# One long convolution and a token mixer on one core: the last step's spectra of x by way of DRAM, the mixer's first statistics inside the convolution's order, and the order itself

## The chip, the cores and the metric

The kernel runs on one core of a Trainium2 chip. A core has four engines that compute: PE (TensorE) multiplies matrices into PSUM, DVE (VectorE), ACT (ScalarE) and POOL (GpSimd) work elementwise. SP (SyncE) issues the DMAs. Each engine takes its instructions in the order in which they stand in its queue and waits on semaphores for the others. The metric is the time of one execution in microseconds (us).

## The reference

```python
def reference(A_u, A_log_A_real, A_A_imag, A_C_real, A_C_imag, A_log_dt, A_D_skip, B_x, B_w1, B_w2, B_w3, B_w4):
    ...
        A = -jnp.exp(log_A_real) + 1j * A_imag
        C = (C_real + 1j * C_imag) * dt[:, None]
        P = jnp.exp((A * dt[:, None])[:, :, None] * pos[None, None, :])
        K = 2.0 * jnp.einsum("dn,dnl->dl", C, P).real
        Kf = jnp.fft.rfft(K, L2)
        Uf = jnp.fft.rfft(u_t, L2)
        y = jnp.fft.irfft(Uf * Kf[None, :, :], L2)[:, :, :L]
        return y + u * D_skip[None, None, :]
    ...
        h = _gelu(_layernorm(x, axis=-1) @ w1)
        ...
        x1 = x + hs
        h2 = _gelu(_layernorm(x1, axis=-1) @ w3) @ w4
        return x1 + h2

    x = A_u
    h = x + _A_ref(_layernorm(x, axis=-1), ...)
    h2 = h + _B_ref(_layernorm(h, axis=-1), ...)
    return h2
```

The sequence has 2048 places and 512 channels, in float32. The first half makes for each channel a filter as long as the sequence out of 128 decaying oscillations, and convolves the normed input with it by Fourier transforms. The second half is a mixer: layer norm, a product with w1, gelu, four shifted groups of channels, a product with w2, then layer norm, w3 (512 to 1792), gelu and w4.

## The kernel before

The convolution (`conv_phase`) goes over the channels in four steps of 128, numbered 0 to 3. Each step has these parts.

- **Tables and taps.** For every 16 channels (32 groups in all, eight a step) `table` makes the oscillations' factors: POOL adds phases (`pt`), ACT takes sines and cosines of them, DVE and POOL multiply with the amplitudes `amx` and `amp` into the tables `cs` and `sn`. `taps` multiplies the tables on PE into `kt`, the taps of the filter. Which group's `amp`, second half of `cs` (`csy`) or of `sn` (`sny`) is POOL's and which is DVE's stands in the table `SHARE`.
- **Spectra of the taps, first stage.** Either `stage_a_turn`, two groups of matmuls (`kt,fas`) for 64 channels and four half transposes on DVE (`at<-bank`, 128x512), or `stage_a_taps`, many small matmuls (`fas,kt`) and copies by ACT. `TURN64` says which 64 channels are turned.
- **Spectra of x, first stage.** `stage_a_x`: matmuls of the normed input h (`h,fas`), and four wide transposes on DVE (`at<-bank`, 128x1024). Once x of a step is read, four DMAs load the raw input into its place in h again, for the residual.
- **Second stage and product.** The buffer `at` has two halves, of x and of the taps. In steps 0 to 2 `product` takes both through the second stage at once, eight times (`at,tbs` into `bank`, 128x256): ACT copies x's spectrum into `xs`, and DVE multiplies it with the taps' spectrum into `u`. In step 3 `spectrum_x` takes x alone ahead of the taps (`at,tbs` 128x128), and ACT keeps the eight results in `xs`, in `scratch` and in `p8`; `product` then takes the taps alone. In step 3 DVE also adds the products in pairs (`u<-u`), so that the inverse takes two terms and not four.
- **The way back.** `stage_b_inv` (`u,ms`, then a copy into `at` by ACT, eight times), `turn_inv` (four transposes on DVE), `stage_a_inv` (`u,fis`), which adds the old h either on PE, by a matmul with the identity (`h,ident`), and lets ACT copy the sum, or on DVE. The last step ends in `last_a_inv`: four pieces of 512 rows, `at,fis` on PE, added into h by DVE, in the order 3, 0, 1, 2.

x of all steps is normed once, in the head (`norm_x`): DVE takes 5 of 16 rows, ACT 11.

What sets the order: every operation goes with a cost, its keys read and written, and for some a due time (`at=`) to a planner, `Plan`. It walks through a model of the engines and always starts what can start first, among equals what is due first. The due times come from the numbers `NOM`. PSUM banks are given out by the planner as well, and where PE would be idle long, it places dummy matmuls with the identity (`filler`). The planner's result is a fixed order for each engine; on the chip each queue runs in this order. SP's DMAs are ordered by it too.

The mixer's phase stands behind it in written order: `finish(3)` takes the statistics of the last 512 rows' second half, `norms([3])` their root by a dozen short DVE operations, `norm1(3)` makes the normed rows `xl`, PE runs nine dummy matmuls (`warm`) and transposes `xl` (`xt`), and then come the products `l` with w1. Its end is a loop over 14 blocks of w3 and w4.

All instructions bear the line of a recording helper (L88 before, L87 after), so that the profile is read by tile names.

Of the kernel before, what the change touches and what calls it, by code (L numbers as in the profile page):

```python
# [287 lines left out]

@with_exitstack
def conv_phase(ctx, tc, cst, tp, h, x, log_A_real, A_imag, C_real, C_imag, log_dt, D_skip, w1, w2, fa, fi, tb, mm_):  # L290
# [422 lines left out]
    def stage_a_x(s, r):  # L713
# [47 lines left out]

    def spectrum_x(s, e):
        n = 4 * WID[s]
        dst, keys = slot(s, e)
# [4 lines left out]
        add("ACT", 0.22 + n * 0.51e-3, lambda: act.copy(dst[:, 0:n], plan.view(p)[:, 0:n]), w=keys, frees=p)

    def product(s, e):
# [735 lines left out]
```

## Time and profile before

| | us |
|---|---|
| median of 3 runs | 735.42 (733.86 to 735.68) |
| the profiled execution | 735.98, span 734.1 |
| convolution, to the mixer's first product | 338.5 |
| the mixer from there | 395.6 |
| busy over the span: PE, DVE, ACT, POOL | 677.4, 543.9, 411.9, 354.6 |

A row of a timeline has its start and length in us, the engine, the line, the operation, out<-in, the shapes and how often it follows itself; in brackets stands how long the engine was idle before it, and what ended that. A row of groups has the count, busy us, mean ns of one, and idle time before. One matmul of float32 is recorded as two rows, so that x16 is eight instructions.

### The profile page before, as it was taken

The page shows a single profiled execution, that of the slowest core. Times are in us where ns is not written, and L with a number is a line of the kernel's source. Part 1 is how long each engine was busy: PE and PEld are TensorE (multiplying, and loading weights), DVE is VectorE, ACT ScalarE, POOL GpSimd, SP SyncE. Part 2 cuts the span into 40 slices and gives each one's busy share as a digit, 9 for nine tenths or more (in the row PEclk, how much of TensorE's full clock was granted, in tenths as well). Part 3 has the DMA queues.
Part 4 walks back from the last instruction along what each step waited for, and adds up shares of the span by engine and source line. Part 5 has one row for each costly group of instructions (what it writes and reads, how often), then busy time and mean ns, then how long its engine had stood idle before and what let it go on. Part 6 is the DMA issues. An engine that isn't in the chain of part 4 may idle for free.

```text
span 734.1 us, 17022 instructions
## 1 busy us (share of the span) xinstructions
PE 677.4 (92%) x7096; PEld 523.4 (71%) x7096; DVE 543.9 (74%) x954; ACT 411.9 (56%) x710; POOL 354.6 (48%) x345
## 2 busy tenths in 40 slices
PE   1997599899988988998999999999999999999997
PEld 1886457537635761867888777888888888888886
DVE  5999899988898988669645689765657965445444
ACT  7687878868966872324744436573535554343430
POOL 0797677477785635001245533543345655444410
PEclk9999789999998998999999999999999999999999
DMA  7920020002001102201001101211122152111014
GB/s 182 312 85 17 3 59 3 17 3 60 18 2 40 25 15 59 59 1 58 1 1 29 30 1 30 71 44 46 41 57 58 45 148 82 47 54 45 13 29 115
DMA packets 40365, 36.82 MB, mean 50 GB/s; under 512 B 4448, under 2 KB 31072, under 8 KB 40288
## 3 DMA queue, kind: packets, MB, share of 16 engines
q1 hardware_dynamic: 39520, 34.68, 17.2%
q10 hardware_dynamic: 768, 1.05, 0.6%
q8 instruction: 56, 0.92, 0.5%
q14 instruction: 21, 0.17, 0.1%
HBM read 31.53 MB, written 4.19 MB: 49 GB/s over the span
## 4 chain that ended last, share of the span: by engine, by line
PE 63%; DVE 15%; ACT 13%; issue 3%; DMA 3%; SPq 1%; POOL 1%; ACTq 0%; DVEq 0%; POOLq 0%
PE l L88 19%; PE bank L88 14%; PE acc L88 10%; ACT pt L88 8%; DVE u L88 3%; DVE sn L88 3%; DVE cs L88 2%; PE l3c L88 2%; PE l3f L88 2%; PE l3d L88 2%; PE l3g L88 2%; PE l3e L88 2%; PE l3a L88 2%; PE l3b L88 2%; DVE at L88 1%
## 5 line engine op out<-in xcount | busy, mean ns | idle before, releaser
L88 ACT ACTIVATE pt<-pt 128x1056 f32<-128x1056 int32 x64 | 69.5, 1086 | 15.2 <-DVE cs L88 8.2
L88 POOL TENSOR_TENSOR pt<-p,s 128x1024 int32<-128x1024 int32 x32 | 63.5, 1989 | 23.8 <-DVE sn L88 20.0
L88 PE MATMUL bank<-at,tbs 128*64 128x256 f32 (+1 forms) x640 | 61.0, 339 | 4.0 <-ACT at L88 3.4
L88 PE MATMUL bank<-u,ms 64*128 64x128 f32 x896 | 56.7, 278 | 3.6 <-DVE u L88 3.3
L88 PEld LDWEIGHTS bank<-u,ms 64*128 64x128 f32 x896 | 52.0, 188 | 7.7 <-DVE u L88 4.9
L88 PEld LDWEIGHTS bank<-at,tbs 128*64 128x64 f32 x640 | 39.2, 134 | 22.4 <-ACT at L88 5.3
L88 PEld LDWEIGHTS bank<-ident 128*128 128x128 f32 x362 | 46.8, 209 | 5.6 <-issue 3.1
L88 PE MATMUL bank<-ident 128*128 128x128 f32 x362 | 50.5, 297 | 0.0
L88 DVE TENSOR_TENSOR cs<-pt,amx 128x512 f32<-128x512 f32 x64 | 41.3, 679 | 6.1 <-ACT pt L88 3.3
L88 DVE TENSOR_TENSOR h<-h,l 128x512 f32<-128x512 f32 x48 | 32.6, 686 | 14.9 <-PE l L88 14.8
L88 DVE TENSOR_TENSOR u<-u,l3f 128x512 f32<-128x512 f32 x14 | 9.6, 684 | 44.9 <-PE l3f L88 44.9
L88 POOL TENSOR_TENSOR cs0w<-raw,cs0w 128x512 fp32r<-128x512 f32 x7 | 9.1, 1301 | 67.0 <-ACT cs0w L88 58.3
L88 POOL TENSOR_TENSOR cs<-pt,amp 128x512 f32<-128x512 f32 x26 | 31.7, 1220 | 16.1 <-ACT pt L88 13.5
L88 POOL TENSOR_TENSOR cs1w<-raw,cs1w 128x512 fp32r<-128x512 f32 x7 | 9.1, 1297 | 61.5 <-ACT cs1w L88 61.5
L88 PE MATMUL bank<-sn 128*32 128x64 f32 x1024 | 32.0, 223 | 6.9 <-DVE sn L88 6.3
L88 ACT ACTIVATE pt<-pt,halfpi 128x1056 f32<-128x1056 f32 x32 | 37.8, 1182 | 0.2
L88 DVE TENSOR_TENSOR u<-xs,bank 128x1024 f32<-128x1024 f32 x26 | 31.5, 1216 | 8.3 <-ACT xs L88 8.0
L88 DVE STREAM_TRANSPOSE at<-bank 128x512 f32<-128x512 f32 (+1 forms) x36 | 33.0, 947 | 6.4 <-PE bank L88 6.3
L88 ACT COPY at<-bank 128x512 f32<-128x512 f32 x44 | 26.7, 616 | 19.2 <-PE bank L88 19.0
L88 ACT ACTIVATE u<-u 128x512 f32<-128x512 f32 x56 | 35.4, 633 | 1.8
L88 PE MATMUL bank<-cs 128*32 128x64 f32 x1024 | 33.2, 225 | 2.8 <-issue 1.1
L88 PEld LDWEIGHTS bank<-cs 128*32 128x32 f32 x1024 | 24.2, 111 | 16.0 <-issue 6.8
(1155 smaller groups left out, 2093.2 us busy)
## 6 DMA issues: line engine op xcount, KB each, us to landing
raw<-in_B_w_dram SPq DMA_DIRECT2D x28, 256.0 KB, 2.8
h<-in_A_u_dram SPq DMA_DIRECT2D x32, 128.0 KB, 4.0
h<-in_A_u_dram SPq DMA_DIRECT2D x16, 256.0 KB, 4.5
rawa<-in_B_w_dram SPq DMA_DIRECT2D x14, 256.0 KB, 2.9
rawb<-in_B_w_dram SPq DMA_DIRECT2D x14, 256.0 KB, 2.9
ms<-in_mm_dram SPq DMA_DIRECT2D x4, 768.0 KB, 11.0
out_dram<-h SPq DMA_DIRECT2D x48, 64.0 KB, 1.7
tbs<-in_tb_dram SPq DMA_DIRECT2D x4, 512.0 KB, 6.5
```

Source lines behind the costliest of these rows:

```text
L88: ins = f(*args, **kw)
```

## The change

Six things change in the convolution.

1. `FAR = [3]`: step 3's x is transformed (`stage_a_x`, then `spectrum_x` eight times) in the head, between the norm and step 0's x. ACT copies each spectrum into one of four buffers (`xs`, `u`, by turns), and a DMA of 256 KB stores it in DRAM (`far`). `back` loads it into the place in `xs`, `scratch` or `p8` from which step 3 multiplies.
2. The sums of products, so far made in step 3 alone, are made for single products of steps 0, 1 and 2 too, on DVE or on POOL (`sum0` to `sum3` in `SHARE`): fifteen in all and not eight, eight of them on POOL.
3. `TURN64` becomes `turn` in `SHARE`: seven of eight groups of 64 channels are turned, and not five. `HADD` becomes `hadd` by halves of a step: half of step 2 has its h added on PE and copied by ACT.
4. `KEEP`: in the last step the old h goes into the sum by identity matmuls ahead of `at,fis`, and ACT copies the four pieces of h; DVE added them before.
5. The statistics of the last 512 rows and their root (`norms`, now a function that both phases use) are handed to the planner.
6. `SHARE` and `NOM` have new numbers, so that the order is another on every engine.

```diff
-SHARE = {'amy': [[2, 5, 6, 7], [0, 1, 2, 3, 4, 5, 7]], 'csy': [[1, 3, 4, 6, 7], [0, 1, 2, 3, 4, 5, 7]], 'sny': [[1, 3, 4, 6, 7], [0, 4, 6, 7]], 'sq': [[1, 4, 5, 7], [0, 2, 4, 6]]}
+SHARE = {'amy': [[2, 3, 5, 6, 7], [0, 1, 2, 3, 4, 5, 6, 7]], 'csy': [[1, 3, 4, 7], [0, 1, 2, 3, 4, 5, 7]], 'sny': [[1, 3, 4, 7], [0, 2, 4, 6, 7]], 'sq': [[0, 1, 2, 7], [1, 2, 3, 4, 6]], 'turn': [[0, 1, 2, 4, 5, 6, 7], [1, 6, 7]], 'hadd': [[0, 1, 2, 3, 5, 7], [0, 2, 5, 7]], 'sum0': [[0], [0]], 'sum1': [[2, 4], []], 'sum2': [[4], [1, 2, 4, 6]], 'sum3': [[0, 1, 2, 3, 5, 6, 7], [1, 4, 7]]}
...
+FAR = [3]
...
-TURN64 = [[0], [0], [0], [0, 1]]
...
-HADD = [True, True, False]
-AHEAD = 8
-KEEP = False
+KEEP = True
...
+def norms(nc, cst, qs):
+
+    ra, rb, rr, nb = cst["norm"]
+    mv, t = cst["mv"], slice(qs[0] * 4, qs[-1] * 4 + 4)
+    return [
+        lambda: nc.vector.tensor_scalar(ra[:, 0, t], mv[:, t, 1], EPS, None, ALU.add),
...
+        *rsqrt_ops(nc, None, None, rr[:, :, t], ra[:, :, t], rb[:, :, t]),
...
+    dpool = pool("far", 1, space=bass.MemoryType.DRAM)
...
+    far = {(s, e): dpool.tile([128, 4 * W], F32, name=f"far{s}{e}") for s in FAR for e in RE}
+
     def spectrum_x(s, e):
         n = 4 * WID[s]
+        k = e % 4
+        dst, keys = (xs[k], [("xs", k)]) if k < XS else (uu[k - XS], [("u", k - XS)])
+        p = add("PE", 0.02 + n * 1.97e-3, lambda: stage_b(s, e, 0, plan.view(p)), dense=DB,
+                r=[("a0", e, q) for q in range(8)] + [("tb", e // 2)], w=keys, bank=1, at=NOM["xa"] + NOM["xs"] * FAR.index(s) + 16 + 2 * e)
+        add("ACT", 0.22 + n * 0.51e-3, lambda: act.copy(dst[:, 0:n], plan.view(p)[:, 0:n]), w=keys, frees=p)
+        add("SP", 0.8, dma(far[s, e][:, 0:n], dst[:, 0:n]), r=keys, w=[("far", s, e)])
+
+    def back(s, e):
+        n = 4 * WID[s]
         dst, keys = slot(s, e)
...
+        add("SP", 0.8, dma(dst[:, 0:n], far[s, e][:, 0:n]), r=[("far", s, e)], w=keys, at=TS[s] + e * NOM["b"] * WID[s] / 128 - 20)
...
+        eng = "POOL" if e in SHARE[f"sum{s}"][1] else "DVE" if e in SHARE[f"sum{s}"][0] else None
...
+            add(eng, 2 * dve(2 * w_) if eng == "DVE" else 1.3, sums, w=[uk], port=True)
...
+        summed = any(e in c for c in SHARE[f"sum{s}"])
+        terms = ((0, 0), (2, 1)) if summed else ((0, 0), (1, 3), (2, 1), (2, 2))
...
+    for n, s in enumerate(FAR):
+        for r in range(WID[s] // 32):
+            stage_a_x(s, r, NOM["xa"] + NOM["xs"] * n)
+        for e in RE:
+            spectrum_x(s, e)
     for r in range(WID[0] // 32):
-        stage_a_x(0, r)
+        stage_a_x(0, r, TS[0] - NOM["ax"])
...
-        for e in range(AHEAD) if last else ():
-            spectrum_x(s, e)
+        for e in RE if last else ():
+            back(s, e)
...
+    add("DVE", 1.8, lambda: finish(3), r=[("hq", 3)] + [("bs", j) for j in range(12, 16)], w=["mv"], at=TS[NS])
+    add("DVE", 2.75, norm_h, r=["mv"], w=["norm"], at=TS[NS])
+    plan.filler = busy
+    plan.run()
...
-    finish(3), norms([3])
     nc.scalar.activation(zero, zero, AF.Gelu_apprx_tanh)
```

The order of the instructions at three places, before and now.

SP's queue in the head, behind the loads of the constants `fis`, `tbs` and `ms`; `ec` is the load of a quarter of w1, h the reload of raw input. Before:

```order
L331 DMA fis<-in_fi_dram 128x64
L331 DMA tbs<-in_tb_dram 128x1024 x4
L331 DMA ms<-in_mm_dram 128x3x512 x4
L331 DMA ec<-in_B_w_dram 128x4x128
L331 DMA h<-in_A_u_dram 32x16x128 x4
```

Now:

```order
L344 DMA ms<-in_mm_dram 128x3x512 x4
L344 DMA ec<-in_B_w_dram 128x4x128
L344 DMA h<-in_A_u_dram 32x16x128 x2
L344 DMA far_125<-xs_123 128x512
L344 DMA far_127<-u_121 128x512
L344 DMA h<-in_A_u_dram 32x16x128
L344 DMA far_124<-xs_122 128x512
L344 DMA far_126<-u_120 128x512
L344 DMA h<-in_A_u_dram 32x16x128
L344 DMA far_129<-xs_123 128x512
L344 DMA far_131<-u_121 128x512
L344 DMA far_128<-xs_122 128x512
```

Eight stores (four from each pair of buffers, `far_130` follows) stand on the queue among the four reloads of step 3's h, where only step 0's reloads stood.

DVE at the end of the last step (`u` the products and their sums, `mvh` the moments of h). Before:

```order
L88 TENSOR_TENSOR u_118<-u_118 128x256 x2
L88 TENSOR_TENSOR u_119<-p_106,bank_81 128x1024
L88 TENSOR_TENSOR u_119<-u_119 128x256 x2
L88 TENSOR_TENSOR u_118<-p_106,bank_82 128x1024
L88 TENSOR_TENSOR u_118<-u_118 128x256 x2
L88 STREAM_TRANSPOSE at<-at 128x16x2x32 x4
L88 TENSOR_TENSOR h<-h,bank_81 128x4x128
L88 TENSOR_TENSOR h<-h,bank_82 128x4x128
L88 TENSOR_TENSOR h<-h,bank_81 128x4x128
L88 TENSOR_TENSOR h<-h,bank_82 128x4x128
L88 BN_STATS bs<-h 128x6 x4
L88 BN_AGGR mvh<-bs 128x2 x4
```

Now:

```order
L87 TENSOR_TENSOR u_121<-u_121 128x256 x2
L87 TENSOR_TENSOR u_120<-scratch,bank_84 128x1024
L87 TENSOR_TENSOR u_121<-p_108,bank_83 128x1024
L87 TENSOR_TENSOR u_120<-p_108,bank_83 128x1024
L87 TENSOR_TENSOR u_120<-u_120 128x256 x2
L87 STREAM_TRANSPOSE at<-at 128x16x2x32 x4
L87 BN_STATS bs<-h 128x6 x4
L87 BN_AGGR mvh<-bs 128x2 x4
```

The four adds of h have left DVE, and two of the last four products have no sums behind them there (POOL makes them). ACT has the copies of h, behind its last copies into `at`; it loaded its next function table there before. Now on ACT:

```order
L87 COPY h<-bank_83 128x16x32
L87 COPY at<-bank_81 128x4x64x2 x8
L87 COPY h<-bank_84 128x4x128
L87 COPY h<-bank_83 128x4x128
L87 COPY h<-bank_82 128x4x128
L87 COPY h<-bank_81 128x4x128
L87 ACT_TABLE_LOAD
L87 ACTIVATE zero<-zero 128x1
```

More of the change, by code (lines that the diff above doesn't have):

```diff
@@ L706, in spectra_of_taps @@
         for r in range(WID[s] // 64):
-            if r in TURN64[s]:
+            if 2 * s + r in SHARE["turn"][0]:
                 stage_a_turn(s, r)
@@ L727, in stage_a_x @@
         keys = [("a0", e, c) for e in RE for c in (2 * r, 2 * r + 1)]
-        p = add("PE", 1.2, mm, dense=0.9, r=[("h", s, r), "fas"] + prm(s), w=keys, bank=2, at=TS[s] - NOM["ax"] + 3.5 * r)
+        p = add("PE", 1.2, mm, dense=0.9, r=[("h", s, r), "fas"] + prm(0), w=keys, bank=2, at=nom + 3.5 * r)
         add("DVE", 1.15, tr, w=keys, frees=p)
@@ L776, in product @@
         a1 = [("a1", q, j) for q in range(w_ // 32) for j in range(2)]
-        if s + 1 == NS and e < AHEAD:
+        if s in FAR:
             p = add("PE", 0.02 + n * 1.97e-3, lambda: stage_b(s, e, 1, plan.view(p)), dense=DB, r=a1 + [("tb", e // 2)],
@@ L804, in product @@
         add("DVE", 0.07 + 2 * n * 1.1e-3, mult, r=keys, w=[uk], frees=p)
-        if s + 1 == NS and e >= YE:
+        eng = "POOL" if e in SHARE[f"sum{s}"][1] else "DVE" if e in SHARE[f"sum{s}"][0] else None
+        if eng:
+            en = gp if eng == "POOL" else v
             q = u[:, 0 : 2 * n].rearrange("p (i n) -> p i n", i=4)
             def sums():
-                v.tensor_tensor(q[:, 0], q[:, 0], q[:, 3], ALU.subtract)
-                v.tensor_tensor(q[:, 1], q[:, 1], q[:, 2], ALU.add)
-            add("DVE", 2 * dve(2 * w_), sums, w=[uk], port=True)
+                en.tensor_tensor(q[:, 0], q[:, 0], q[:, 3], ALU.subtract)
+                en.tensor_tensor(q[:, 1], q[:, 1], q[:, 2], ALU.add)
+            add(eng, 2 * dve(2 * w_) if eng == "DVE" else 1.3, sums, w=[uk], port=True)
     def stage_b_inv(s, e):
@@ L1006, in conv_phase @@
             weights()
-        for e in range(AHEAD) if last else ():
-            spectrum_x(s, e)
+        for e in RE if last else ():
+            back(s, e)
         for e in RE:
+            if s in FAR and not last:
+                back(s, e)
             product(s, e)
@@ L1015, in conv_phase @@
                 stage_a_inv(s, r)
-            for r in range(WID[s + 1] // 32):
-                stage_a_x(s + 1, r)
+            for r in range(WID[s + 1] // 32) if s + 1 not in FAR else ():
+                stage_a_x(s + 1, r, TS[s + 1] - NOM["ax"])
         else:
@@ L1023, in conv_phase @@
             last_a_inv(s)
-    plan.filler = busy
-    plan.run()
     o = D // 2
@@ L1086, in mixer_phase, with root @@
     mv = cst["mv"]
-    ra, rb, rr, nb = cst["norm"]
+    _, _, rr, nb = cst["norm"]
     r1, r12 = rr[:, 0, :], rr[:, 1, :]
     off1, off12 = nb[:, 0, :], nb[:, 1, :]
-    def norms(qs):
-        t = slice(qs[0] * 4, qs[-1] * 4 + 4)
-        nc.vector.tensor_scalar(ra[:, 0, t], mv[:, t, 1], EPS, None, ALU.add)
-        nc.vector.tensor_scalar(ra[:, 1, t], mv[:, t, 1], 1.0 + EPS, EPS * EPS, ALU.mult, ALU.add)
-        for op in rsqrt_ops(nc, None, None, rr[:, :, t], ra[:, :, t], rb[:, :, t]):
-            op()
-        nc.vector.scalar_tensor_tensor(
-            nb[:, :, t], mv[:, t, 0].unsqueeze(1).to_broadcast([128, 2, len(qs) * 4]), -1.0, rr[:, :, t], ALU.mult, ALU.mult)
+    def root(qs):
+        for op in norms(nc, cst, qs):
+            op()
     def transposed(tiles, name, wide=True, cs=range(4)):
```

33 lines of the change are left out of this document (17 added, 16 removed).

## The prediction

> **What bounds the kernel now.** I read the slices of the page first, then busy time and granted clock by stage, then the chain of waits, then each engine's timeline at the stage ends. Busy time by stage: start and end in us, length, then busy us (and instructions) of PE, its weight load, DVE, ACT and POOL, granted clock, DMA share, GB/s.
>
> ```profile
> 75.00:102.00 27.00, 19.00 (x430) 10.69 (x422) 24.23 (x49) 21.28 (x33) 18.33 (x16) 0.75 0.18 38
> 102.00:274.00 172.00, 157.01 (x3282) 106.14 (x3282) 154.67 (x228) 133.44 (x229) 116.14 (x98) 0.98 0.09 20
> 274.00:297.50 23.50, 21.62 (x345) 7.31 (x336) 18.64 (x23) 6.44 (x13) 10.07 (x8) 0.85 0.34 82
> 297.50:319.70 22.20, 22.20 (x339) 19.73 (x336) 15.85 (x24) 8.39 (x15) 0.00 (x0) 1.00 0.06 11
> 319.70:338.50 18.80, 15.30 (x111) 10.74 (x109) 15.42 (x43) 3.89 (x6) 0.10 (x1) 0.91 0.19 57
> 338.50:734.10 395.60, 389.33 (x1758) 320.27 (x1756) 250.07 (x442) 183.46 (x312) 165.54 (x175) 1.00 0.16 46
> ```
>
> The convolution (to 338.5) is not bound by one engine. From 102 to 274 DVE is busy 154.7 of 172 us, 90%, in an order that no other engine can hurry; PE's 157 holds fillers. From 297.5 to 319.7 PE has no gap, while DVE has 6 us free. The mixer is PE's: 389 of 395.6. The chain of waits, pieces in order of time (start, us, what), says the same of the last step:
>
> ```profile
> 287.63 31.99 PE bank L88 x447
> ```
>
> Thirty-two us of PE alone, up to the turns of the last step. So an edit before 274 is priced in DVE time, one in the last step in PE time, and what the mixer's start gains reaches the end whole, since the mixer's instructions are not touched.
>
> **DVE work ahead of the last table.** The last table (its two products into `cs`) ends at 273.65 + 1.28 = 274.9:
>
> ```profile
> 273.65 1.28 DVE L88 TENSOR_TENSOR cs<-pt,amx 128x512 f32<-128x512 f32 x2
> 297.56 1.22 DVE L88 TENSOR_TENSOR u<-xs,bank 128x1024 f32<-128x1024 f32 x1 [1.88 <-ACT xs L88]
> 319.72 4.63 DVE L88 STREAM_TRANSPOSE at<-at 128x1024 f32<-128x1024 f32 x4 [1.73 <-ACT at L88]
> 325.87 0.69 DVE L88 TENSOR_TENSOR h<-h,bank 128x512 f32<-128x512 f32 x1 [1.52 <-PE bank L88]
> 329.30 0.69 DVE L88 TENSOR_TENSOR h<-h,bank 128x512 f32<-128x512 f32 x1 [0.45 <-PE bank L88]
> 329.90 1.40 DVE L88 BATCH_NORM_STATS2 bs<-h 128x6 f32<-128x256 f32 x4
> ```
>
> I counted DVE's instructions ahead of that point in both orders, by shape, and took the differences times the mean of each group (count, busy us, mean ns):
>
> ```profile
> L88 DVE STREAM_TRANSPOSE at<-bank 128x1024 f32<-128x1024 f32 x16 | 19.6, 1249 | 5.7 <-PE bank L88 5.6
> L88 DVE STREAM_TRANSPOSE at<-bank 128x512 f32<-128x512 f32 x20 | 13.3, 706 | 0.7 <-PE bank L88 0.7
> L88 DVE TENSOR_TENSOR amp<-E,ec 128x512 f32<-128x512 f32 x7 | 6.4, 913 | 0.0
> L88 DVE TENSOR_TENSOR amx<-E,amx 128x896 f32<-128x896 f32 x16 | 17.4, 1088 | 2.3 <-ACT amx L88 2.2
> L88 DVE TENSOR_TENSOR amx<-E,amx 128x512 f32<-128x512 f32 x16 | 11.1, 691 | 0.9 <-ACT amx L88 0.7
> L88 DVE TENSOR_TENSOR cs<-pt,amp 128x512 f32<-128x512 f32 x6 | 5.8, 974 | 0.0
> L88 DVE TENSOR_TENSOR sn<-pt,amp 128x512 f32<-128x512 f32 x15 | 11.3, 751 | 0.0
> L88 DVE TENSOR_TENSOR u<-u 128x256 f32<-128x256 f32 x16 | 6.1, 421 | 0.3
> ```
>
> Added: the four transposes of the last step's x, 4 x 1.25 = 5.0; two more 64-channel turns of taps ahead of this point, 8 x 0.71 = 5.6; two sums, 4 x 0.42 = 1.7; one `cs` half, 1.0. Removed: four `amp`, 3.7; three wide `amx` for narrow ones, 3 x 0.40 = 1.2; two `sn` halves, 1.5. Net **+7.0 us**, on the path, because DVE is the bound there. What those edits spare the others (8 of ACT's copies into `at`, PE's small matmuls of taps, and half of the inverse matmuls of seven products) hides under DVE and counts nothing.
>
> **The head and the trip through DRAM.** The last step's eight spectra now come between the norm of x and step 0, in the same buffer `at`, so that step 0's x cannot be turned before they are read.
>
> ```profile
> 79.06 7.86 ACT L88 ACTIVATE h<-h,bs 128x512 f32<-128x512 f32 x11
> L88 ACT COPY xs<-bank 128x512 f32<-128x512 f32 x26 | 15.0, 579 | 6.3 <-PE bank L88 6.3
> 96.61 1.25 DVE L88 STREAM_TRANSPOSE at<-bank 128x1024 f32<-128x1024 f32 x1 [0.65 <-PE bank L88]
> h<-in_A_u_dram SPq DMA_DIRECT2D x16, 256.0 KB, 4.5
> ec<-in_B_w_dram SPq DMA_DIRECT2D x8, 256.0 KB, 2.8
> out_dram<-h SPq DMA_DIRECT2D x48, 64.0 KB, 1.7
> ```
>
> Before, x of step 0 is turned at 97.9, 11 us after ACT's last norm. In the new order thirteen short DVE operations have left the place ahead of the norm, worth some 2.6 us, so x of step 3 is turned at about 95. Then four spectra (on PE 0.95 each, a sixth of the 5.67 quoted further down, the last copy 0.6 and some waiting later), a store that must land before its buffer is written again, the other spectra (1.9) and the first of step 0's transforms (1.3): 4.8 + 0.5 of issue + landing + 3.4, that is 11.5 us if a store lands in 2.8, as a load of that size does, and 13.2 at 4.5, the row of the reloads of h that stand between the stores on SP's queue. DVE has 18 instructions, some 9.6 us, meanwhile, so it stalls 1.9 to 3.6 us; the earlier norm pays 2.6. That is -0.7 to +1.0; I take **+1.0**, as nothing here shows eight stores and four reloads together. The return trip is cheap: six of eight loads are issued long before the last step, and the last two, into `xs`, follow step 2's last products, with twelve us of DVE work to cover 2.8 of landing.
>
> **Idle time of DVE from 102 to 274.** It is 17.3 us. One piece goes: the taps of step 2's second 64 channels are turned now, and not made by 128 small matmuls at which PE ran dry:
>
> ```profile
> 229.82 1.07 PE L88 MATMUL bank<-fas,kt 32*64 32x32 f32 x30 [1.36 <-issue]
> 232.96 1.25 DVE L88 STREAM_TRANSPOSE at<-bank 128x1024 f32<-128x1024 f32 x1 [2.75 <-PE bank L88]
> L88 POOL TENSOR_TENSOR p<-p,sh 128x256 int32<-128x256 int32 x7 | 5.0, 721 | 1.0 <-DVE sh L88 0.5
> L88 DVE TENSOR_TENSOR kt<-kt,dsk x8: 173/693/1373, 54.0 to 278.3; 128x16 f32<-128x16 f32 x8
> ```
>
> So -2.75 at most. Against it stand five pairs of sums that POOL now makes in steps 0 to 2: by POOL's nearest row a pair takes 2 x 0.72 = 1.44. A DVE operation of 128x16 takes 0.17 at best and up to 1.37 (minimum, median, maximum in that row), so something holds DVE for about one POOL operation; if every pair held it once, +7.2. DVE mostly reads PSUM here, so I take 1.25: **-1.5**, bounds -2.75 and +4.45.
>
> **From the last table to the last step's first product.** Now 297.56 - 274.9 = 22.6 us, of which PE spent the time from 285 on x of step 3:
>
> ```profile
> 287.63 2.62 PE L88 MATMUL bank<-h,fas 32*32 32x512 f32 x32
> 294.86 5.67 PE L88 MATMUL bank<-at,tbs 128*64 128x128 f32 x96
> 300.46 1.16 PE L88 MATMUL bank<-u,ms 64*128 64x128 f32 x16
> 276.29 1.09 PE L88 MATMUL bank<-kt,fas 32*32 32x512 f32 x16
> 160.62 1.12 PE L88 MATMUL bank<-h,ident 128*128 128x512 f32 x2
> 161.68 1.26 PE L88 MATMUL bank<-u,fis 128*32 128x512 f32 x8
> 324.47 4.76 PE L88 MATMUL bank<-at,fis 128*32 128x512 f32 x32
> 330.13 2.25 PE L88 MATMUL warm<-ident 128*128 128x128 f32 x18 [0.91 <-DVE h L88]
> 334.95 3.79 PE L88 MATMUL xt<-ident,xl 128*128 128x128 f32 x16 [2.58 <-DVE xl L88]
> ```
>
> All of that is gone from this place. What is left on DVE, in the new order: four wide transposes (5.0), eight half ones (5.6), one tap sum (0.7), two adds of h (1.4): 12.7 us. PE's part, four turns at 1.09, three inverse groups at 1.26, one identity at 1.12 and a spectrum at 0.95, sums to 10.2. The first product waits for the last half transpose, 0.7 before the last add's end, and then for its spectrum of 0.95: 13.0 is the floor, and 18, with the old stage's clock of 0.85 and idle time on both engines, the ceiling. I take 14: **-8.6**, bounds -9.6 and -4.6.
>
> **The last step's loop**, 319.72 - 297.56 = 22.2 now. Left on PE: two groups of step 2's last quarter (2.4), seven spectra of taps (7 x 0.95 = 6.6), eight inverse groups (8 x 1.09 = 8.7), two identity matmuls that hold h for the end (2.2), 0.5 for POOL's three sums and 0.9 to the turn: 21.4. **-0.8**: the eight spectra (7.6 us) have left PE, but two of step 2's groups and h's hold have moved in.
>
> **The start of the mixer.** Before, DVE adds all four pieces of h (325.87 to 329.99) and only then takes statistics of the first. Now ACT copies the pieces, and statistics can start one copy after the first: 6.15 + 0.6 + 0.1 after the turns begin, against 10.18. From there to the transposes of `xl` it is 334.95 - 329.90 = 5.05, so `xl` would be there 11.9 after the turns; but PE's `warm` still waits for the last piece (10.4) and takes 2.25, so that they start at 12.66, and not at 15.23: **-2.6**.
>
> **Sum**: +7.0 + 1.0 - 1.5 - 8.6 - 0.8 - 2.6 = -5.5. The profiled execution took 735.98 (span 734.1 and 1.9 around it), 0.56 above the median of 735.42. So 730.5 as that execution, and **729.9** as a median.
>
> **Rivals.**
> *The last step frees more.* If the chain after the last table is the floor of 12.9 and PE's dry runs vanish from step 0 too, the sum loses another 1.0 + 1.25 + 2 (such a run as step 2's is 2.75): about 725.6. For it: step 0's taps lose the same small matmuls. Against: the head hides them.
> *The gain is only half.* The chain stays at 18 us since turn, tap sum, PE and copy wait for each other as now: -5.5 + 4 = -1.5, 733.9, no change that can be told (under 0.3%, 2.2 us, a measurement cannot tell).
> *POOL's sums hold DVE (slower).* Place: steps 0 to 2, five pairs; POOL's queue is in order, so a pair that waits for DVE's product also holds back the next phases, and ACT and DVE behind these. At 2.9 us a pair (1.44 each of holding and of delay) it costs 14.5 in place of 1.25: 729.9 + 13.2 = 743; it decides from 1.8 us a pair. For it: the 1.37 row. Against: POOL is idle a third of that stage. [...]
> *Stores that land late (slower).* If a store among reloads takes three times the reloads' 4.5, the head stalls 8.7 + 13.5 - 9.6 - 2.6 = 10.0 in place of 1.0: 738.9; it decides from a landing of 12.3. [...] The quoted stores of the output, 64 KB, land in 1.7 us, which speaks against it.
>
> **How the numbers follow.** The forecast (gain of 2.2 to 9) 0.52, more freed 0.18, half the gain 0.15, slower 0.15 (POOL 0.09, stores 0.06). Hence faster 0.70, within 0.3% 0.15, slower 0.15. All best bounds with step 0's dry run give -11.6, 723.8; all worst ones without the two slower rivals +4.5, 739.9. The range is 723 to 738: it leaves out the worst of POOL and of the stores.
>
> **What would show it.** In the new trace: the last table's end at 281 or so (+6.5); from there to the first product into `u` of the last step about 14 us, with no `h,fas` on PE; 21 us to the turns; statistics of the first piece 7 us after the turns begin. In the head, PE waiting for a DMA of `far` between its two halves of four spectra by 2 us. I am wrong if the last table ends past 286 (POOL or the stores), or if the stretch after it does not shrink.

## The result, and the profile after

The changed kernel takes **723.96 us** (median of 4 runs, 723.78 to 724.35) against 735.55 before (4 runs, 733.86 to 738.21): ratio 0.984, 95% interval 0.981 to 0.987. The gain is 11.6 us, more than twice the forecast 5.5. Three more measurements on other occasions gave 721.28, 721.47 and 722.20, ratios of 0.979 to 0.981. The profiled execution took 724.12, span 722.3.

Busy time by stage of the changed kernel, the stages cut as before (norm of x to the first product; to the last table's end; to the last step's first product; to its turns; to the mixer's first product; the rest):

```profile
74.15:111.82 37.67, 27.10 (x454) 15.55 (x454) 33.84 (x56) 27.70 (x46) 23.15 (x21) 0.86 0.37 109
111.82:275.88 164.06, 148.31 (x2946) 94.49 (x2942) 151.25 (x225) 130.03 (x224) 124.79 (x110) 0.99 0.14 34
275.88:289.92 14.04, 11.58 (x155) 3.45 (x156) 11.48 (x16) 5.10 (x9) 10.39 (x9) 0.88 0.30 78
289.92:311.45 21.53, 21.53 (x258) 15.38 (x258) 13.58 (x19) 5.42 (x9) 4.28 (x6) 1.00 0.01 2
311.45:326.66 15.21, 13.93 (x103) 9.10 (x102) 12.32 (x39) 6.35 (x11) 0.10 (x1) 1.00 0.23 69
326.66:722.34 395.68, 389.40 (x1756) 320.13 (x1756) 250.51 (x442) 182.93 (x311) 165.68 (x175) 1.00 0.17 46
```

The marks, from the timelines of DVE and PE:

```profile
275.19 0.68 DVE L87 TENSOR_TENSOR cs<-pt,amx 128x512 f32<-128x512 f32 x1
289.92 1.22 DVE L87 TENSOR_TENSOR u<-xs,bank 128x1024 f32<-128x1024 f32 x1 [2.56 <-PE bank L87]
311.45 4.62 DVE L87 STREAM_TRANSPOSE at<-at 128x1024 f32<-128x1024 f32 x4 [2.90 <-ACT at L87]
318.38 1.42 DVE L87 BATCH_NORM_STATS2 bs<-h 128x6 f32<-128x256 f32 x4 [2.30 <-ACT h L87]
321.81 2.27 PE L87 MATMUL warm<-ident 128*128 128x128 f32 x18 [0.71 <-ACT h L87]
323.92 2.18 PE L87 MATMUL xt<-ident,xl 128*128 128x128 f32 x16
```

The last table ends at 275.9 and not at 281: that is the miss. Behind it nearly everything stands where it was put: 14.0 us to the first product, 21.5 to the turns, 12.5 from there to the transposes.

How DVE reached the last table, busy time from the span's start, before and after (columns as above: DVE's is the third pair):

```profile
0.00:274.93 274.93, 229.85 (x4604) 165.92 (x4608) 244.87 (x426) 209.79 (x367) 178.94 (x161) 0.95 0.21 56
```
```profile
0.00:275.87 275.87, 228.06 (x4252) 158.21 (x4252) 248.64 (x437) 212.75 (x375) 190.40 (x176) 0.97 0.27 75
```

Idle time is length less busy time: 30.1, now 27.2. Busy time I split again. For each form of DVE instruction I took the fastest tenth of its rows in both profiles as its own time (0.42 for `u<-u` 128x256, 0.18 for `kt<-kt,dsk`), and what a row took beyond it by over 0.1 as waiting inside the instruction: 16.2 us in 27 rows before, 12.8 in 29 rows now. The rest is work: 228.7 before, 235.8 now. How the fastest tenth is taken moves such a sum of waits by some tenths of a us, and by 1 us at most, so that their fall is 2.8 to 3.4.

| us | forecast | measured | changed kernel, second profile (span 719.2) |
|---|---|---|---|
| DVE's work to the last table | +7.0 | +7.1 | +7.3 |
| DVE's idle time to there | +1.0 - 2.75 | -2.8 | -3.9 |
| waits inside DVE's instructions | +1.25 | -3.4 | -4.0 |
| last table to first product | -8.6 | -8.6 | -10.0 |
| last step's loop | -0.8 | -0.6 | -0.6 |
| turns to the mixer's transposes | -2.6 | -2.8 | -2.8 |
| transposes to the first mixer product | 0 | -0.8 | -0.8 |
| the mixer | 0 | 0.0 | -0.2 |
| sum | -5.5 | -11.8 | -15.0 |

What these waits are, in the head of the kernel before (timeline, DVE and POOL together):

```profile
82.25 3.96 POOL L88 TENSOR_TENSOR pt<-p,s 128x1024 int32<-128x1024 int32 x2
82.37 2.03 DVE L88 SCALAR_TENSOR_TENSOR scratch<-scratch 128x128 f32<-128x128 f32 x1
84.33 2.13 DVE L88 TENSOR_SCALAR scratch<-ec 128x256 f32<-128x256 f32 x1
```

Two DVE instructions of 0.28 and 0.46 us own time take 2.03 and 2.13: each starts just after one of POOL's and ends 0.15 to 0.25 us behind its end. Nearly all of the 27 long rows before (the exceptions are transposes, with some 0.1 us) start while an instruction of POOL runs and end after it. Of the 16.2 us, 10.7 lay ahead of the first product (now 6.2 ahead of a first product that comes ten us later). Two transposes from PSUM in the changed kernel took 1.26 and 1.29 us beside POOL's 3.89, where the mean of the sixteen is 1.26, so that these were not held:

```profile
85.37 3.89 POOL L87 TENSOR_TENSOR pt<-p,s 128x1024 int32<-128x1024 int32 x2
86.16 1.26 DVE L87 STREAM_TRANSPOSE at<-bank 128x1024 f32<-128x1024 f32 x1 [0.46 <-PE bank L87]
87.69 1.29 DVE L87 STREAM_TRANSPOSE at<-bank 128x1024 f32<-128x1024 f32 x1 [0.27 <-PE bank L87]
```

### The profile page after: what moved, and what is told of

It reads as the page before. It is cut to its first block, busy times and chain, and to the rows that moved or that the text cites. A ratio compares the mean times of both kernels' runs of the same rounds, so it can differ in the third digit from the quotient of the medians.

```text
span 722.3 us, 15951 instructions
## 1 busy us (share of the span) xinstructions
PE 664.5 (92%) x6522; PEld 506.3 (70%) x6522; DVE 536.6 (74%) x949; ACT 412.6 (57%) x714; POOL 370.9 (51%) x366
## 3 DMA queue, kind: packets, MB, share of 16 engines
q10 hardware_dynamic: 768, 1.05, 0.6%
## 4 chain that ended last, share of the span: by engine, by line
PE 63%; DVE 15%; ACT 13%; issue 4%; DMA 2%; POOL 2%; SPq 1%; DVEq 0%; ACTq 0%; POOLq 0%
PE l L87 20%; PE bank L87 13%; PE acc L87 11%; ACT pt L87 7%; PE l3c L87 3%; PE l3f L87 2%; PE l3d L87 2%; PE l3e L87 2%; PE l3g L87 2%; PE l3a L87 2%; PE l3b L87 2%; DVE at L87 2%; DVE u L87 2%; DVE cs L87 2%; ACT E L87 2%
## 5 line engine op out<-in xcount | busy, mean ns | idle before, releaser
L87 PE MATMUL bank<-at,tbs 128*64 128x256 f32 (+1 forms) x640 | 64.0, 345 | 9.9 <-DVE u L87 4.9
L87 POOL TENSOR_TENSOR pt<-p,s 128x1024 int32<-128x1024 int32 x32 | 63.4, 1986 | 14.8 <-DVE sn L87 13.1
L87 PE MATMUL bank<-u,ms 64*128 64x128 f32 x784 | 52.6, 281 | 3.2 <-DVE u L87 1.7
L87 PEld LDWEIGHTS bank<-u,ms 64*128 64x128 f32 x784 | 46.4, 188 | 12.9 <-issue 3.9
L87 DVE TENSOR_TENSOR h<-h,l 128x512 f32<-128x512 f32 x48 | 32.6, 687 | 14.9 <-PE l L87 14.8
L87 PE MATMUL bank<-ident 128*128 128x128 f32 x318 | 42.8, 295 | 0.0
L87 PEld LDWEIGHTS bank<-ident 128*128 128x128 f32 x318 | 40.1, 207 | 3.5 <-issue 2.6
L87 DVE STREAM_TRANSPOSE at<-bank 128x512 f32<-128x512 f32 (+1 forms) x44 | 38.6, 908 | 4.8 <-PE bank L87 4.8
L87 POOL TENSOR_TENSOR amp<-E,ec 128x512 f32<-128x512 f32 x29 | 32.6, 1131 | 14.6 <-DVE ec L87 11.0
L87 DVE TENSOR_TENSOR u<-xs,bank 128x1024 f32<-128x1024 f32 x26 | 31.6, 1216 | 10.4 <-ACT xs L87 5.7
L87 POOL TENSOR_TENSOR h<-h,x 128x512 f32<-128x512 f32 x16 | 22.1, 1388 | 24.7 <-DVE x L87 24.7
```

The source lines that it names most:

```text
L87: ins = f(*args, **kw)
```

## The experiments

The theory after the result: the work was counted right, and what the forecast missed is waiting, inside DVE's instructions and between them, that the changed kernel avoids. Rivals: those instructions are long for another reason; or one part of the change carries the missing 6 us alone. The changed kernel's own medians run from 721.3 to 724.0, so a difference of 3 us or less between two rows rests on their traces or on a run beside it, and not on the medians. All runs at a glance (us; the last table's end; DVE's waits inside, idle time and work up to it; from there to the last step's first product; its loop):

| run | median | table | waits / idle / work | to product | loop |
|---|---|---|---|---|---|
| before | 735.55 | 274.9 | 16.2 / 30.1 / 228.7 | 22.6 | 22.2 |
| changed | 723.96 | 275.9 | 12.8 / 27.2 / 235.8 | 14.0 | 21.5 |
| e9, e14, e16: changed again | 721.28, 721.47, 722.20 | 274.4, 274.7, 274.4 | 12.2 / 26.2 / 236.0 (e9) | 12.6 | 21.5 |
| e1, e10: step 1's sums to PE | 720.29, 719.82 | 272.6, 273.0 | 9.4 / 28.1 / 235.0 (e1) | 12.6, 13.9 | 21.6 |
| e2: POOL's sums to PE | 723.73 | 277.1 | 12.1 / 28.8 / 236.1 | 12.6 | 21.6 |
| e3: h added by DVE | 724.51 | 274.7 | 13.0 / 25.8 / 236.0 | 12.6 | 20.4 |
| e4: POOL busy in the head | 727.46 | 280.6 | 17.4 / 27.4 / 235.8 | 14.0 | 21.6 |
| e5: x of step 3 late | 730.58 | 272.5 | 12.0 / 29.5 / 230.9 | 22.6 | 23.3 |
| e6: old due times | 731.21 | 278.2 | 10.6 / 31.1 / 236.5 | 19.4 | 20.9 |
| e7: before, new engine lists | 736.09 | 270.6 | 13.1 / 34.3 / 223.3 | 30.6 | 21.2 |
| e8: no sums in step 1, new order | 723.18 | 277.0 | 10.4 / 31.7 / 234.9 | 12.4 | 20.9 |
| e11: old turns | 739.22 | 285.7 | 14.2 / 41.0 / 230.6 | 20.0 | 21.6 |
| e12: PE's gaps filled | 721.37 | 274.1 | 12.2 / 25.7 / 236.2 | 12.6 | 21.5 |
| e13: e1 and e12 together | 719.64 | 272.9 | 9.6 / 28.5 / 234.8 | 12.6 | 21.6 |
| e15: e11 with dummies | 749.76 | 294.7 | 15.2 / 49.3 / 230.2 | 19.4 | 21.5 |

**e4, the wait by itself.**

```diff
+            for _ in range(3 if k == 5 else 0):
+                gp.tensor_tensor(uu[0].rearrange("p (a n) -> p a n", n=128), wide, wide, ALU.add)
```

> The changed kernel with three more POOL additions of 128x1024 (about 2 us each, into a buffer that is not in use there) behind the phases' factors at 71.3 us, where POOL is idle for 6.9 us and DVE runs short instructions on SBUF until the norm; nothing else is moved, and no result depends on them. Theory A (a DVE instruction on SBUF that meets one of POOL's waits until that ends, which is the 10.7 us that the kernel before lost inside DVE's instructions in its head): DVE gets one short instruction in for each addition, the norm starts about 5 us later, the last table ends about 5 later, and the kernel takes 727 to 729. Theory B (such instructions are long for another reason, and an idle POOL can be filled for nothing): 724.

Measured 727.46 (0.9878, 0.9834 to 0.9922). Timeline of the head, and then the same three instructions in the changed kernel:

```profile
71.28 5.93 POOL L87 TENSOR_TENSOR u<-ident 128x1024 f32<-128x1024 f32 x3
71.81 1.41 DVE L87 SCALAR_TENSOR_TENSOR bs<-bs 128x16 f32<-128x16 f32 x1
73.37 1.99 DVE L87 TENSOR_TENSOR scratch<-scratch 128x128 f32<-128x128 f32 x1
75.37 1.97 DVE L87 TENSOR_SCALAR scratch<-ec 128x128 f32<-128x128 f32 x1
78.75 5.04 ACT L87 ACTIVATE h<-h,bs 128x512 f32<-128x512 f32 x7 [2.16 <-DVE bs L87]
```
```profile
71.82 0.18 DVE L87 SCALAR_TENSOR_TENSOR bs<-bs 128x16 f32<-128x16 f32 x1
72.15 0.29 DVE L87 TENSOR_TENSOR scratch<-scratch 128x128 f32<-128x128 f32 x1
72.45 0.28 DVE L87 TENSOR_SCALAR scratch<-ec 128x128 f32<-128x128 f32 x1
```

Three short instructions, 0.18, 0.29 and 0.28 us in the changed kernel, take 1.41, 1.99 and 1.97. DVE's waits up to the norm rise from 2.95 to 7.54, its idle time and work stay to within 0.1, and the norm, the last table and the end move by 4.6 to 4.7 against the first profile of the changed kernel, whose two later clock drops (below) this one has at the same places. So filling an idle POOL for 5.9 us cost 4.6 of that execution's time. Theory A holds: the waits are POOL's doing, and those in the head are on the path.

**e1 and e10, step 1's sums left to PE, order kept.** `made` are the terms that are issued; the planner still sees the old ones:

```diff
-            add(eng, 2 * dve(2 * w_) if eng == "DVE" else 1.3, sums, w=[uk], port=True)
+            add(eng, 2 * dve(2 * w_) if eng == "DVE" else 1.3, (lambda: None) if s == 1 else sums, w=[uk], port=True)
...
+        made = four if s == 1 else terms
```

> The changed kernel with the two pair sums of step 1 left to PE (four terms in two inverse products instead of sums by DVE); the order of all other instructions is kept, and what is computed is the same. In the changed kernel's trace these four DVE instructions of 128x256 take 5.0 us, 1.29 each, where the same form takes 0.42 elsewhere, and each ends when a POOL instruction ends. Theory A (they wait for POOL inside their own duration, and without them nobody waits in their place): the last table ends 5.0 sooner, at 270.9, and the kernel takes about 719. Theory B (the wait is POOL's making and goes to the next DVE instruction): only their own work goes, 4 x 0.42 = 1.7, so 722.3. Theory C (PE's two extra products, 2 x 0.92, are on the path): 722.3 + 1.8 = 724.

> The changed kernel without step 1's two pair sums and with the order kept, once more and beside the changed kernel on the same chip. Theory A (the 3.3 us of waits inside DVE's sums are gone, and nothing takes their place): 3.3 to 4.8 below the changed kernel, about 720. Theory B (the 1.5 us of clock between the two were luck, and so was the rest): less than 2 below.

What went, in the changed kernel's groups (count, busy us, mean ns):

```profile
L87 DVE TENSOR_TENSOR u<-u 128x256 f32<-128x256 f32 x4 | 5.0, 1289 | 0.0
```

e1 took 720.29 (0.9788, 0.9752 to 0.9824), e10 719.82 (0.9773, 0.9759 to 0.9787), beside e9 with 721.28 (0.9794, 0.9780 to 0.9808). Waits fell by 2.8 to 3.4 and work by 0.9 to 1.1, but 0.9 to 2.5 came back as idle time, so that the last table is 1.4 to 1.8 sooner than in e9. The forecast had charged these sums 1.7; they took 5.0, and doing without them is worth 1.5: more than no gain, less than theory A's 5, and in e10 less than the 2 of its theory B. The size is near e1's theory B, but not by its mechanism: the waits did go, and idle time took most of their place.

**e2, POOL's sums of steps 0 and 2 left to PE**, the same edit with `s < 3 and s != 1`.

> The changed kernel with the five pair sums that POOL makes in steps 0 and 2 left to PE (four terms); the order of all other instructions is kept, what is computed is the same. POOL's ten instructions take 0.73 each. Theory A (they hold DVE as the forecast's 1.25 us has it, and PE's 5 x 0.92 more lies under DVE): 1.2 us less at most, so 722.8 to 724. Theory B, the forecast's rival (POOL's sums hold DVE by 1.8 us a pair or more): at least 7 us less, 717 or below.

723.73 (0.9835, 0.9800 to 0.9870). POOL's sums are no burden: waits are 0.1 to 0.7 less without them, and idle time is 1.6 more than in the changed kernel's first profile, which has the same clock drop near 207; most likely PE's five longer products are not all hidden. The rival in which they hold DVE is out.

**e3, the old h added by DVE again** (`KEEP = False`).

> The changed kernel with the last step's old h added by DVE again, not by identity matmuls on PE and copies by ACT; the rest of the plan is the changed one. Theory A (the forecast's terms, taken apart): PE loses four identity matmuls in the last step's loop, 2.2 us, but the statistics wait for four adds of h, so that the transposes of the normed rows start 15.2 us after the turns begin and not 12.5: +2.7 - 2.2 = +0.5, 724.5. Theory B (the hold of h costs nothing on PE since the loop waits for DVE and POOL anyway): the loop keeps its 21.5 us and the time is 726.7.

724.51 (0.9846, 0.9809 to 0.9883). PE's timeline in it:

```profile
320.66 3.90 PE L87 MATMUL warm<-ident 128*128 128x128 f32 x18 [3.46 <-DVE h L87]
324.40 1.91 PE L87 MATMUL xt<-ident,xl 128*128 128x128 f32 x16
```

The loop is 1.1 shorter, not 2.2, and the transposes start 16.7 after the turns, not 15.2; but `warm` took 3.90, as the clock was at 0.50 there, where it takes 2.27 above. Without that 1.6, it is 15.1. From the last step's first product to the mixer's, e3 then takes 0.7 more than the changed kernel, near theory A's 0.5, and 2.4 more with the slow `warm`. The slow `warm` followed PE's wait of 3.46 us for DVE's h, so it may belong to this order and not to chance; one profile can't tell. The forecast's term for the start, -2.6, is there (15.1 less 12.5); its 2.2 for holding h in the loop was 1.1.

**e5, x of step 3 in its old place** (`FAR = []`, spectra straight into SBUF, old due times for these two stages).

```diff
-        add("SP", 0.8, dma(far[s, e][:, 0:n], dst[:, 0:n]), r=keys, w=[("far", s, e)])
...
-            back(s, e)
+            spectrum_x(s, e)
...
-                stage_a_x(s + 1, r, TS[s + 1] - NOM["ax"])
+                stage_a_x(s + 1, r, TS[s + 1] - (-54.92 if s + 1 in LATE else NOM["ax"]))
```

> The changed kernel with step 3's x transformed in its old place: turned after step 2, its eight spectra made on PE ahead of the last step's products and kept in SBUF, nothing sent to DRAM; all other parts of the change stay, the planner orders anew. Theory A (this part only moves work out of the last step): the stretch from the last table to the turns grows by 9.2 (44.8 before, 35.6 now), DVE has four wide transposes less ahead of the last table, 4 x 1.16 = 4.6, and the head's stall for the stores, 1.1, goes: +3.5, 727.5. Theory B (the new head, with x of step 3 in it, is also what keeps DVE from meeting POOL there): the 4.5 us of waits inside DVE's instructions in the head come back as well, 732.

730.58 (0.9931, 0.9908 to 0.9954). From the last table to the first product, and the loop:

```profile
272.46:295.03 22.57, 20.35 (x276) 7.22 (x276) 15.61 (x21) 6.33 (x11) 9.25 (x8) 0.92 0.37 87
295.03:318.36 23.33, 23.33 (x332) 19.06 (x326) 13.57 (x19) 8.32 (x14) 4.26 (x6) 1.00 0.05 9
```

Against the changed kernel's first profile, 10.3 us come back here (22.6 is the old figure), 5.0 of DVE's work go, idle time grows by 2.3. The waits inside did not come back (12.0; 3.8 up to the first product), so theory B's mechanism is out, though the time lies nearer to its figure. The store and reload cost little: in the changed kernel `far` lands in 2.7 us in the median and 3.7 at most, and DVE's idle time from norm to first product grew by 1.1.

**e6, the changed kernel with the old due times** (`NOM` of before, `xa` and `xs` kept).

> The changed kernel with the due times of the kernel before (the numbers NOM; the two new ones for the head's x stay). The amount of work is the same on every engine. DVE's order is the same for its first 230 rows, up to the end of step 0. Theory A (the due times have no part in what the head gained; the norm starts at 74.2 and the waits inside DVE's instructions up to the first product stay at 6.2 us): the price lies behind step 0 alone, in idle time of DVE, 2 to 5 us, 726 to 729. Theory B (the new due times carry the missing 6 us of the gain): 730 or more.

731.21 (0.9927, 0.9901 to 0.9953). The head is unchanged (norm at 74.4, waits 6.6 up to the first product), as theory A has it, but the price is theory B's. It lies in the stretch after the last table, where PE and DVE wait for each other and the clock is low (0.82):

```profile
278.19:297.64 19.45, 15.08 (x168) 5.20 (x170) 11.24 (x17) 5.46 (x10) 10.44 (x9) 0.82 0.23 63
```
```profile
290.56 1.38 PE L87 MATMUL bank<-h,ident 128*128 128x512 f32 x2 [2.20 <-DVE at L87]
```
```profile
283.61 2.40 DVE L87 STREAM_TRANSPOSE u<-at 128x1024 f32<-128x1024 f32 x2 [2.52 <-ACT at L87]
297.64 1.22 DVE L87 TENSOR_TENSOR u<-xs,bank 128x1024 f32<-128x1024 f32 x1 [5.36 <-PE bank L87]
```

19.4 in place of 12.6 to 14.0, and 3.8 to 4.9 of idle time before. The edits allow the short stretch; the order makes it.

**e7, the kernel before with the four new engine lists** (`amy`, `csy`, `sny`, `sq`).

> The kernel before with nothing but the four lists of the tables' engines (amp, second halves of cs and sn, and the short form of amx) from the changed one; the planner orders anew, due times are the old ones. Theory A (these lists bring the head's gain: fewer DVE instructions that meet POOL's, so that waits inside DVE's instructions ahead of the norm and the first product fall from 10.7 to about 6): DVE has 4.6 us less work ahead of the last table (four amp and two sn halves less, one cs half more, 0.68 each, and three short forms more, 0.4 each) and 4.5 us less waiting, 9 in all less what comes back as idle time: 727 to 731. Theory B (it takes the whole new order): DVE's work is less but its idle time grows by as much, 734 to 737.

736.09 (0.9999, 0.9978 to 1.0021): nothing. The last table ends 4.4 sooner (work -5.5, waits -3.1, of it -2.9 ahead of the norm, idle +4.2), and the stretch behind it gives that back: 30.6, of which two products of step 2 that are now behind the table are a part.

```profile
270.56:301.16 30.60, 26.18 (x382) 12.00 (x378) 20.71 (x24) 6.90 (x13) 7.90 (x7) 0.89 0.25 62
```

So the engine lists alone free DVE ahead of the norm, as in the changed kernel, and gain nothing without an order that uses it.

**e8, no sums in step 1, planned anew** (`'sum1': [[], []]`).

> The changed kernel without pair sums in step 1, as in the run that left them to PE, but with the planner told of it, so that it orders anew from there. Theory A (the planner's model of the shared time of DVE and POOL places DVE's instructions as well as the kept order does): 720.3 as with the kept order, within 1.5. Theory B (a new order finds other meetings of DVE and POOL): up to the 5 us that the sums cost in either direction from 722.

723.18 (0.9830, 0.9808 to 0.9852), 3 us over the kept order. The waits are no worse (10.4 against 9.4), idle time is (31.7 against 28.1): the planner's model is not good to 3 us.

**e11, the old turns; e15, the same with dummy matmuls.**

```diff
-'turn': [[0, 1, 2, 4, 5, 6, 7], [1, 6, 7]]
+'turn': [[0, 2, 4, 6, 7], [1, 6, 7]]
```
```diff
+                    if q % 4 == 3:
+                        busy(plan.view(ids[jp])[:, 0, 256:512])
```

> The changed kernel with the turned groups of taps as before: the second 64 channels of steps 0 and 2 go by 256 small matmuls each on PE and four copies by ACT, instead of four half transposes on DVE; the planner orders anew. Theory A (by the forecast's terms): DVE has 8 x 0.62 = 5.0 less to do ahead of the last table, PE runs dry for 2.75 in step 2 again, and the sum is -2.2: 721.8. Theory B (more idle time than that goes with the turns: DVE's idle time from the first product to the last table fell by 4.5 in the change and not by 2.75, and step 0's small matmuls stand in the head): the idle time comes back with 5 or more and the time is 724 to 727.

> The kernel with the old turned groups, and two dummy matmuls with the identity (128x128) in each group of 64 rows of small matmuls of taps, 24 in all, about 0.23 us each; the order of all else is kept. Theory A (the small matmuls of 32x32 let the granted clock fall to half, and PE is then the bound for as long as it lasts): the half clock from 158 to 175 is gone or shorter by 7 us and more, and the time falls by 6 to 9, to 730 to 733, though PE has 5 us more to do. Theory B (PE is late for other reasons and the clock only follows): the same stretch of half clock and the same 739, or up to 5 more.

e11 took 739.22 (1.0031, 1.0009 to 1.0053): undoing two of eight groups costs 17.9 and takes the whole gain, which is past both theories. DVE's work falls by 5.5, as the forecast has it, but its idle time to the last table rises by 14.8, and 7.5 more are lost behind. The worst place is the change from step 0 to step 1:

```profile
160.00:170.00 10.00, 10.00 (x214) 5.85 (x218) 4.25 (x5) 5.69 (x9) 7.64 (x7) 0.50 0.01 2
170.00:180.00 10.00, 10.00 (x76) 1.86 (x68) 6.55 (x8) 3.18 (x8) 1.18 (x2) 0.74 0.01 2
```
```profile
167.50 1.25 DVE L87 STREAM_TRANSPOSE u<-at 128x1024 f32<-128x1024 f32 x1 [4.64 <-PE bank L87]
```

PE is busy without a gap, at half clock, and DVE waits. In e15 the clock is whole at this place:

```profile
160.00:170.00 10.00, 10.00 (x224) 5.86 (x224) 6.02 (x9) 3.60 (x7) 7.32 (x6) 1.00 0.12 29
170.00:180.00 10.00, 10.00 (x140) 3.33 (x136) 7.68 (x9) 5.95 (x11) 2.98 (x3) 1.00 0.01 2
```

but the run took 749.76 (1.0194, 1.0136 to 1.0252), past both theories again. From the first product to here it gained some 3 us on e11; the head lost 3.8, and more was lost later. Nor is it shown that the dummies made the clock whole. In step 2 the same small matmuls stand, in e15 with dummies and in e11 without (e15 first):

```profile
241.60:251.80 10.20, 10.20 (x122) 4.79 (x124) 4.90 (x7) 5.96 (x12) 2.99 (x4) 0.50 0.01 2
```
```profile
236.00:246.00 10.00, 9.54 (x310) 4.88 (x314) 7.89 (x13) 8.94 (x16) 4.52 (x4) 1.00 0.01 3
```

There the clock was at half with the dummies and whole without them. If those 3 us are the price of e11's half clock near 160, some 15 of the 17.9 are left, and no run explains them. Nor is the figure a price of the turns alone, since the due times were fitted to the others.

**e9, e12, e13, e14, e16: what is 1.5 us between executions.** e12 puts two dummy matmuls behind each of step 2's first two inverse groups:

```diff
+            for _ in range(2 if s == 2 and r < 2 else 0):
+                busy(amx.rearrange("p d i -> p (d i)")[:, 0:512])
```

> The changed kernel once more, beside the next one. Theory A (the 14.0 us from the last table to the last step's first product in its first profile hold 1.5 us of a lower granted clock, 0.65 from 286 to 289.6, as the runs without sums show 12.6 there): either 14.0 or 12.6 there, 722.3 to 724.3 in all. Theory B (the stretch is 14.0 in the changed kernel always): 14.0 again.

> The changed kernel with four dummy matmuls with the identity (two behind each of the first two inverse groups of step 2) in PE's gaps after the last table, where PE waits 0.96 and 0.73 us for DVE's transposes; all else is kept. Theory A (the gaps make the granted clock fall in some executions, 0.65 from 286 to 289.6, and that costs 1.5 us): the stretch takes 12.6 in the profile, and the executions lie within 1 us of each other at the lower end of the changed kernel's, 720.9 to 721.7. Theory B (the clock falls for another reason): 14.0 or 12.6 as before, and the spread of 1.6 us stays.

> The same dummy matmuls in the kernel that leaves step 1's pair sums to PE with the order kept. Theory A (the sums cost 4 x 0.42 of work and 2.8 us of waits inside, of which idle time gives back 2.2, so that about 1.5 is left, and the clock costs another 1.5 in some executions): 719.2 to 719.8, 1.5 below the run with the dummies alone. Theory B (the 3.3 us of waits are gained whole): 717.5 to 718.5.

> The changed kernel beside these two on one chip. Theory A: 721 to 722.6, by the clock after the last table. Theory B (chips differ by more than that): anywhere from 720 to 724.5, and only the differences within this group count.

> The changed kernel beside it on the same chip, for the difference: 721 to 724 as in its other runs; by both theories the same.

The first profile of the changed kernel and the one of e9, by the same windows:

```profile
207.00:211.00 4.00, 4.00 (x32) 2.29 (x30) 3.17 (x5) 1.29 (x3) 1.07 (x1) 0.62 0.00 0
286.00:290.00 4.00, 4.00 (x27) 1.26 (x26) 1.45 (x4) 0.66 (x2) 1.28 (x1) 0.68 0.02 4
```
```profile
207.00:211.00 4.00, 4.00 (x90) 3.16 (x90) 4.00 (x7) 2.62 (x5) 1.07 (x1) 1.00 0.01 4
286.00:290.00 4.00, 4.00 (x42) 2.01 (x40) 1.22 (x1) 1.13 (x2) 1.45 (x2) 1.00 0.01 4
```

One kernel, one order; in e9 the clock is whole from 88 us to 719. With the two drops the last table is 1.5 later and the stretch behind it 1.5 longer: DVE's rows fall behind e9's from 210 to 214 us and again by 290, and hardly anywhere else. That is the whole of 722.3 against 719.2. The 14.0 is thus not there always, as e9's theory B had it, and e9 came out below the 722.3 of its theory A because the first drop, near 207, was missing too. The dummies did not narrow the spread, as e12's theory B has it: it took 721.37, but one of its runs 722.97, a spread as wide as in e14 beside it (721.35 to 722.83). e13 took 719.64 (0.9771, 0.9755 to 0.9786) against 721.47 in e14 (0.9801, 0.9784 to 0.9817) and 1.7 below e12, as its theory A has it. The versions without step 1's sums, e10 and e13, beat both kernels, by 1.5 and 1.8 us over the changed one beside them; in e13's case no two runs overlap.

## Why the prediction was wrong

The direction was right, and 723.96 lies in the range, 1 us above its lower end; but the gain is twice the forecast's. Of six terms four fit to half a microsecond or better.

- *DVE's work, +7.0*: +7.1. Right, though the two sums in it, priced 1.7, took 5.0 with what they waited.
- *Head and DRAM, +1.0*: DVE's idle time up to the first product grew by 1.7. The norm came 4.9 earlier, not 2.6: ahead of it DVE had 2.7 less work, which is the forecast's figure, and 2.9 less waiting inside instructions (5.8 before, 2.9 now), less 0.6 of idle time. No wait of PE for a `far` DMA is seen between the two halves of four spectra: tables and dummies stand there. The late stores are out.
- *Idle time of DVE in the middle, -2.75*: -4.5, and in e9 -5.8. The dry run of step 2 is gone, as are smaller waits for `at<-bank`. The forecast read this run as PE running dry; but before, the clock was at 0.50 from 230 to 234 us and PE busy throughout, so that part of the 2.75 was a slow PE, and no run shows how much. *POOL's sums, +1.25*: no run shows this term. The forecast took one hold of five since DVE "mostly reads PSUM here", but before only 40 of its 228 instructions from 102 to 274 did, and that such rows are spared was then its author's estimate. Waits inside DVE's instructions in the middle grew by 1.2, which is luck: e2 shows that it wasn't POOL's sums (0.1 to 0.7 less without them), and e1 that most of it was at DVE's own in step 1.
- **The step that failed** is the one that puts the last table at 281: "Net +7.0 us, on the path", with DVE's waits taken over from before but for one dry run. The table came 5.6 us sooner than that sum has it: 4.65 by waits inside DVE's instructions (-3.4 and not +1.25), 1.05 by idle time, nothing by work. The forecast read waiting only where DVE was idle. It saw 1.37 us in the row of `kt<-kt,dsk`, used it to price POOL's new sums, and did not ask how much of before's busy time was of this kind: 16.2 us. Of these 4.5 went ahead of the first product, and 1.2 came back in the middle. That waits are POOL's and cost their full length ahead of the norm, where 2.9 of the 4.5 went, is shown by e4; behind the norm the share is an account of the two traces, and e1 warns that waits taken away there come back in part as idle time.
- *Last table to first product, -8.6*: -8.6, and -10.0 without the clock drop, so that the exact fit is luck. The floor of 13.0 was undercut: 12.6. Part of the gain here is the clock's: over this stretch it was 0.85 before, 0.88 in the first profile and 1.00 in e9. e5 shows that x's move is needed for it, and e6 that the order is too.
- *Loop, -0.8*: -0.6. *Start of the mixer, -2.6*: -2.8, and 0.8 more behind it, since the 16 transposes take 2.18 and not 3.79: before, the profile had the clock at 0.57 from 335 to 339.

Of the rivals "the last step frees more", at 725.6, was nearest. Its shorter stretch came in the profiles without a drop; whether step 0's dry runs went as it says was not separated from the rest. "POOL's sums hold DVE" had the mechanism that decided, at the wrong instructions and with the wrong sign: such waits were already being paid, and the change lowered the bill by some 3 us.

What stays open: which edit lowered it between the norm and the first product (ahead of the norm the engine lists suffice, e7), how much of the gain is the clock's, and why undoing single parts costs 6 to 18 us where the whole brings 12 to 15. e5, e6, e7 and e11 say only that the parts don't add up: each was planned with the others.

## What to carry to other kernels

Before busy time of an engine is taken as work, compare each group's mean with its fastest row, and see whether the longer rows end with another engine's: what is above was a wait here (e4), and another division of the work between the two engines can lower it, as e7's lists did by 2.9 us ahead of the norm (there without a gain in the whole time). When an order is planned, price a change by the new order's own rows, as the stretch behind the last table was here, and don't expect one part undone to give that part's price. In e4 an idle POOL was not free for work while DVE ran from SBUF to SBUF: 5.9 us of additions cost 4.6.

## What the runs showed of the hardware

*The clock's grid.* In all 18 profiles of this case the granted clock is either half or whole, and each stretch at one of them lasts a multiple of 3.41 us (the last is cut off by the end); where this grid lies against the program differs from one execution to the next. The changed kernel's drop near 207, with the 3.41 us ahead of it, and then e9 over the same work:

```profile
203.22:206.63 3.41, 1.64 (x18) 1.25 (x20) 3.41 (x5) 1.68 (x4) 2.35 (x2) 1.00 0.03 10
206.63:210.05 3.42, 3.42 (x18) 1.58 (x16) 3.14 (x5) 0.34 (x2) 1.07 (x1) 0.50 0.00 0
```
```profile
204.15:207.56 3.41, 2.19 (x26) 1.50 (x26) 3.41 (x5) 0.86 (x2) 1.52 (x2) 1.00 0.00 0
```

PE was busy for 1.64 of 3.41 us ahead of the drop, and its longest wait in the 10 us before was 1.07 us; in e9 the grid lies 0.8 us later against the work, the window has 2.19 of 3.41, and the clock stays whole. Counted over the 18 profiles from 60 to 345 us, by such windows at whole clock: with PE busy for less than half of the window, 36 of 37 were followed by half clock; with 50 to 62%, nine of 49; with 62 to 75%, none of 122; with more, four of 1195. So a window that is half idle was enough here. Ahead of the changed kernel's second drop PE was busy for 2.05 of 3.41 us, where both happen; the grid's place may thus be all that parts 719.2 from 722.3, but this is a count of windows, and no run moves PE's share alone.

*Small matmuls.* The four windows with a busy PE (in e5, e7 and twice in e15) all hold dozens of matmuls of 32x32. In e11 the clock stayed at half from 158 to 175 us while PE's busy share was full (10.00 of 10.00 us from 160 to 170, at 0.50), with such matmuls among its work. Dummies of 128x128 between them were no remedy that can be counted on: in e15 the clock was whole in step 0 (1.00 from 160 to 180), where e11 had the half, and at half for 10.2 us in step 2 (0.50 from 241.6 to 251.8), where e11 had the whole (1.00 from 236 to 246).
